# One accumulator for three float passes, and another order of the first units

## The chip, the cores and the metric

The kernel runs on one core of one Trainium2 chip. The metric is the time of one execution in microseconds (us), as the device counts it. Its parts are called by the names of the profile: PE is the matrix engine and PEld its weight loads, ACT, DVE and POOL are the engines that work element by element, SP issues nearly all the DMA transfers.

## The reference

A decaying linear attention over `q`, `k`, `v` (batch 4, 8 heads, 768 tokens, 64 columns a head) is worked in blocks of 64 tokens, with a state that runs from block to block. Its result, seen as 3072 tokens of 512 values, goes through two dense layers with a leaky rectifier between:

```
x = attn_out.transpose(0, 2, 1, 3).reshape(B * S, H * D)   # 3072 x 512
h = x @ w_in                                               # 512 x 2048
g = np.maximum(0.01 * h, h)
return (g @ w_out).astype(np.float32)                      # 2048 x 512
```

The two weight matrices arrive as 8-byte floats, the rest as 4-byte floats.

## The kernel before, in words

**Precision by three passes.** Every dense product is worked in three matmul passes over operands of a short float type. An operand `x` is cut into `xh` (rounded), `xl` (the rest) and `xm`; a weight is cut into `wh`, `wl` and `wm` the same way (`parts`, L587 to L598, and `difference`, L600). The passes are called h, l and m. With S = 4096, the product is (S+1) times (hh + ll), plus mm, all over S times U. So the sum of the first two passes must be multiplied by S+1 before or after the third is joined to it.

**Stage 1** (`up`, L628) works for a group `g` of 4 chunks of 128 tokens and one of 8 slices `p` of 256 columns of `w_in`: a unit `("up", g, p)`. A unit has two blocks of 128 columns, and a block has 4 matmuls of 512 columns for each pass, so a unit has 24 matmuls. Passes h and l add up in one bank of the accumulator memory (L655, L656). Then ACT multiplies the bank in place by S+1 (L658), pass m is added (L660), and ACT takes the bank through the leaky rectifier into `gs` (L661), which a DMA writes to memory (L664). The blocks go round two banks at first and then three, `b10`, `b11`, `b2`.

**Stage 2** (`down`, L688) reads those results back (`down_load`, L673: ACT L682, DVE L683 and L685 make the three parts), and for each group and each of its 4 blocks of 128 tokens (`tb`) adds up 16 slices of 128. Passes h and l go to one bank and pass m to another, so that the 4 blocks fill all 8 banks (`acc`, L668). At the end ACT takes the first bank into `tt`, scaled (L722), and DVE adds the second to it (L729). The output rows are written by L732. The last block of all takes its m pass in two halves of 256 columns, so that the first half can be emptied early.

**Attention** runs in rounds `("r", c)`, one for each chunk: transposes (L403), scores and states (L313 into `psc`), outputs (L313 into `po`), with DVE (L452, L459), POOL (L419, L423, L462) and ACT (L414, L415, L491) between. Its results become `xh` (ACT L507), `xl` and `xm` (DVE L508, L510).

**Weights.** `("wi", p)` loads one slice of `w_in` in two halves of 512 KB each (L566), and turns 8-byte floats into 4-byte floats in the one buffer `w32`: ACT L578, L580 and L582, DVE L584 and L585 for each half. `parts` then makes `wh` (ACT L591 or DVE L593, whichever the planner finds), `wl` (DVE L596) and `wm` (DVE L602). The next slice may be written to `w32` by L578 once the last reader of `w32` is through; before, that reader is `wl`, since `wm` is made of `wl` and `wh`. `w_out` goes the same way during stage 1, is parked in memory, and is cut into parts near the end of stage 1.

**The order.** `seq` (L738) is a list written out by hand for the first 41 entries, and made by loops afterwards. Its place in the list is an operation's rank. A planner (`Plan.emit`, L83) gives each operation a start by hand-written costs: whatever can start first goes first, and ranks decide between equals. Keys (the strings in `add`) carry the reads and writes between operations, in the order of `seq`. Each engine then runs its own instructions in the planned order and waits at the first that isn't ready. While the first units are not there yet, `busy` (L263) fills PE's idle time with transposes of an identity.

Of the kernel before, what the change touches and what calls it, by code (L numbers as in the profile page):

```python
# [8 lines left out]
F32 = mybir.dt.float32  # L9
# [6 lines left out]
ALU = mybir.AluOpType  # L16
# [9 lines left out]
S = 4096.0  # L26
NEAR = 1.0 - 2.0 ** -13
U = 16.0
WS = S * U
# [133 lines left out]
def kernel(  # L163
# [65 lines left out]
    tt = [raw[-1][:, i * T:(i + 1) * T] for i in range(2)]  # L229
# [357 lines left out]
    def parts(p, src, keys):  # L587
        wh, wl, wm = W[p]
        def head(e):
            if e == "ACT":  # L590
                nc.scalar.activation(out=wh, in_=src, func=AF.Copy, bias=0.0, scale=NEAR / S)  # L591
            else:
                nc.vector.tensor_scalar(wh, src, NEAR / S, None, op0=ALU.mult)  # L593

        add(("ACT", "DVE"), (1.05, 0.7), head, keys, [f"wh{p}"])
        add("DVE", 1.25, lambda: nc.vector.scalar_tensor_tensor(wl, wh.bitcast(F32), -S, src, op0=ALU.mult, op1=ALU.add),  # L596
            keys + [f"wh{p}"], [f"wl{p}"])
        difference(p)  # L598

    def difference(p):  # L600
        wh, wl, wm = W[p]
        add("DVE", 1.25, lambda: nc.vector.scalar_tensor_tensor(wm, wl.bitcast(F32), 1.0, wh.bitcast(F32), op0=ALU.mult, op1=ALU.subtract),  # L602
            [f"wh{p}", f"wl{p}"], [f"wm{p}"])
# [24 lines left out]
    def up(g, p, lo=0, hi=GC):  # L628
# [20 lines left out]
        for fs in blocks:  # L649
            kb = ("b10", "b2")[n_b % 2] if n_b < 0 else ("b10", "b11", "b2")[n_b % 3]  # L650
            n_b += 1
            b = bank[kb][:, :len(fs) * n].rearrange("p (f t) -> p f t", f=len(fs))
            r = y[:, fs[0]:fs[-1] + 1, :]
            for i, f in enumerate(fs):
                add("PE", us, lambda f=f, d=b[:, i, :], first=i == 0: product(d, f, 0, first), keys("h"), [kb])  # L655
                add("PE", us, lambda f=f, d=b[:, i, :]: product(d, f, 1), keys("l"), [kb])  # L656
            ns = 0.6 if len(fs) * n == T else 0.4
            add("ACT", ns, lambda b=b: nc.scalar.activation(out=b, in_=b, func=AF.Copy, bias=0.0, scale=S + 1.0), [], [kb], rank=-1.5)  # L658
            for i, f in enumerate(fs):
                add("PE", us, lambda f=f, d=b[:, i, :]: product(d, f, 2), keys("m"), [kb])  # L660
            add("ACT", ns, lambda b=b, r=r: nc.scalar.activation(out=r, in_=b, func=AF.Prelu, bias=0.0, scale=1.0 / WS, alpha=0.01),  # L661
                [kb], [f"gs{jg}"], rank=-1.5)
# [5 lines left out]
    acc = [[z[:, i].rearrange("p y t -> p (y t)") for i in range(2)] for z in (psc, po)] + [  # L668
        [b1[0], b2], [b1[1], pt.rearrange("p y t -> p (y t)")]]
    ACC = [["psc", "psc"], ["po", "po"], ["b10", "b2"], ["b11", "pt"]]  # L670
# [17 lines left out]
    def down(g, p):  # L688

        nonlocal n_t  # L690
        for tb in range(GC):
            done = p + 2 == NP
            very_last = done and g == NG - 1 and tb == GC - 1

            def go(pps, zs, cols, tb=tb):
                for pp in pps:
                    j = (g * NP + pp) % NR
                    for f in range(2):
                        for z in zs:
                            nc.tensor.matmul(acc[tb][z // 2][:, cols], lhsT=ring[j][z][:, f * T + tb * P:f * T + (tb + 1) * P],  # L700
                                             rhs=W[pp][z][:, f * d_model:(f + 1) * d_model][:, cols],
                                             start=pp == 0 and f == 0 and z != 1, stop=pp == NP - 1 and f == 1,
# [4 lines left out]

# [7 lines left out]
            for pps, zs, cols in order:  # L715
                part_of = f"{halves.index(cols)}" if cols in halves else ""
                add("PE", 0.227 * 2 * len(pps) * len(zs) * (0.53 if part_of else 1.0), lambda pps=pps, zs=zs, cols=cols, go=go: go(pps, zs, cols),
                    needs(pps, ["hlm"[z] for z in zs]) + ([ACC[tb][1]] if part_of else []), sorted({ACC[tb][z // 2] + part_of for z in zs}))
            if done:
                jt, n_t = n_t % 2, n_t + 1  # L720
                t, y = tt[jt], gs[jt][:, 0, :]
                add("ACT", 0.6, lambda t=t, tb=tb: nc.scalar.activation(out=t, in_=acc[tb][0], func=AF.Copy, bias=0.0, scale=(1.0 + 1.0 / S) / U),  # L722
                    [ACC[tb][0]], [f"t{jt}"], rank=-1.5)
                rows = out[(g * GC + tb) * P:(g * GC + tb + 1) * P, :]
                n = 2 if very_last else 1
                for i in range(n):
                    cols = slice(i * d_model // n, (i + 1) * d_model // n)
                    add("DVE", 0.69 / n + 0.08 * (n - 1),
                        lambda t=t, y=y, tb=tb, cols=cols: nc.vector.scalar_tensor_tensor(  # L729
                            y[:, cols], acc[tb][1][:, cols], 1.0 / WS, t[:, cols], op0=ALU.mult, op1=ALU.add),  # L730
                        [f"t{jt}", ACC[tb][1]] + ([ACC[tb][1] + str(i)] if n == 2 else []), [f"gs{jt}{i}" if n == 2 else f"gs{jt}"], rank=-1.5)
                    add("DMA", 0.8 / n, lambda rows=rows, y=y, cols=cols: nc.sync.dma_start(out=rows[:, cols], in_=y[:, cols]),  # L732
                        [f"gs{jt}{i}" if n == 2 else f"gs{jt}"], [], rank=-1.5)
# [4 lines left out]
    seq = [("a", 0), ("a", 1), ("a", 2), ("a", 3), ("wi", 1), ("b", 4), ("r", 4), ("up", 0, 1), ("wi", 0), ("r", 5),  # L738
# [24 lines left out]
    for n, x in enumerate(seq):  # L763
# [15 lines left out]
        elif x[0] == "wp":  # L779
            if not freed:  # L780
                add("DVE", 0.0, lambda: None, [], ATT + [f"gr{j}" for j in range(NR)])
                add("ACT", 0.0, lambda: None, [], [f"raw{j}" for j in range(NRAW)] + ["t0", "t1"])
# [38 lines left out]
```

## Time and profile before

| | |
|---|---|
| time, median of 3 runs | 612.35 us (611.60 to 612.74) |
| span of the profiled execution, first to last instruction | 609.2 us; no other time of that execution is recorded |
| mean granted TensorE clock | 0.999 |
| PE busy | 597.9 us, 5386 matmuls |
| ACT busy | 269.0 us, of it L658 56.1 us in 97 instructions |
| DVE busy | 314.0 us |
| first unit of stage 1 begins | 28.67 us |
| first matmul of stage 2 begins | about 343.5 us |
| last matmul ends | 605.62 us |

A profile row gives a line of the kernel, an engine and an operation with its tiles, how often it ran, its busy time and the mean of one, and behind the bar how long the engine stood idle before it and who ended that. "128x512" is 128 partitions by 512 elements. A matmul's record lasts longer than the step from one matmul to the next, since matmuls are pipelined; the step is what counts for the time.

### The profile page before, as it was taken

Reading aid. Unit: us, or ns where it says so; the run is one execution under the profiler, and the core shown is the slowest. Engines: PE = TensorE matmul, PEld = TensorE weight load, DVE = VectorE, ACT = ScalarE, POOL = GpSimd, SP = SyncE. Lnnn points to the kernel's source line nnn. Section 1 sums busy time; section 2 is a strip of 40 time slices with the busy share of each in tenths; the row PEclk is TensorE's granted clock in tenths of the full one; section 3 lists DMA queues with packets and bytes.
Section 4 is the critical chain, followed back from the end, with each engine's and each line's share of the span. In section 5 each row is a group of like instructions: output and inputs, shape, how many; then the busy total and the mean of one; then the engine's idle time right before and its main releaser. Section 6 shows DMA issues by size and latency. Waiting matters only on the chain.

```text
span 609.2 us, 12932 instructions
## 1 busy us (share of the span) xinstructions
PE 597.9 (98%) x5386; PEld 495.6 (81%) x5386; DVE 314.0 (52%) x418; ACT 269.0 (44%) x430; POOL 86.8 (14%) x90
## 2 busy tenths in 40 slices
PE   7899999999999999999999999999999999999997
PEld 6687888888888878888788888888888888888886
DVE  5999764334243426326366745545454544635531
ACT  4688974444455646555577522222222313214111
POOL 1654412104133004104000000000000000000000
PEclk9999999999999999999999999999999999999999
DMA  9998774667888878886686843524333343333201
GB/s 213 232 272 245 221 203 124 173 133 199 199 213 238 212 227 214 216 244 210 233 300 217 290 145 103 173 69 139 138 104 131 112 138 105 138 104 122 86 1 69
DMA packets 147754, 105.18 MB, mean 173 GB/s; under 512 B 123632, under 2 KB 124400, under 8 KB 147696
## 3 DMA queue, kind: packets, MB, share of 16 engines
q1 hardware_dynamic: 147552, 104.36, 58.9%
q8 instruction: 42, 0.69, 0.5%
q14 instruction: 16, 0.13, 0.1%
q10 hardware_dynamic: 144, 0.00, 0.0%
HBM read 68.69 MB, written 35.65 MB: 171 GB/s over the span
## 4 chain that ended last, share of the span: by engine, by line
PE 92%; DVE 4%; DMA 2%; ACT 1%; issue 0%; POOL 0%; SPq 0%; DVEq 0%; ACTq 0%
PE b L640 40%; PE b L700 18%; PE po L700 11%; PE psc L700 11%; PE po L313 4%; PE pt L700 4%; PE psc L313 4%; DMA g<-gs 1%; DMA att<-in_v_dram 1%; DVE w L584 1%; DVE w L585 1%; DVE wm L602 1%; PE pt L403 1%; DMA att<-in_k_dram 1%; DVE wl L596 0%; DVE wh L593 0%
## 5 line engine op out<-in xcount | busy, mean ns | idle before, releaser
L682 ACT ACTIVATE xh<-att 128x1024 fp32r<-128x1024 f32 x48 | 50.7, 1060 | 148.7 <-PE b L700 140.7
L683 DVE SCALAR_TENSOR_TENSOR xl<-att,xh 128x1024 fp32r<-128x1024 f32 x48 | 58.6, 1223 | 98.6 <-ACT xh L682 98.6
L640 PE MATMUL b<-xm,wm 128*128 128x512 f32 (+2 forms) x392 | 104.5, 393 | 0.5 <-ACT b L658 0.5
L640 PE MATMUL b<-xl,wl 128*128 128x512 f32 (+2 forms) x392 | 103.4, 388 | 0.6 <-DVE wl L596 0.6
L640 PE MATMUL b<-xh,wh 128*128 128x512 f32 (+2 forms) x392 | 103.2, 387 | 0.8 <-ACT xh L507 0.8
L640 PEld LDWEIGHTS b<-xh,wh 128*128 128x128 f32 x392 | 73.0, 188 | 15.9 <-ACT xh L507 0.9
L640 PEld LDWEIGHTS b<-xl,wl 128*128 128x128 f32 x392 | 72.8, 188 | 15.6 <-DVE wl L596 1.0
L640 PEld LDWEIGHTS b<-xm,wm 128*128 128x128 f32 x392 | 71.5, 188 | 15.7 <-ACT b L658 0.9
L658 ACT ACTIVATE b<-b 128x512 f32<-128x512 f32 (+2 forms) x97 | 56.1, 580 | 60.3 <-PE b L640 60.1
L661 ACT ACTIVATE gs<-b 128x512 f32<-128x512 f32 (+2 forms) x97 | 56.8, 591 | 44.9 <-PE b L640 38.8
L700 PE MATMUL b<-wl,xl 128*128 128x512 f32 x192 | 74.8, 390 | 0.0
L700 PE MATMUL b<-wh,xh 128*128 128x512 f32 x192 | 74.8, 390 | 0.0
L685 DVE SCALAR_TENSOR_TENSOR xm<-xl,xh 128x1024 fp32r<-128x1024 f32 x48 | 58.7, 1226 | 4.7
L462 POOL TENSOR_TENSOR att<-att 128x256 f32<-128x256 f32 x40 | 35.0, 876 | 57.2 <-DVE att L459 55.9
L700 PEld LDWEIGHTS b<-wl,xl 128*128 128x128 f32 x192 | 36.1, 188 | 7.4
L700 PEld LDWEIGHTS b<-wh,xh 128*128 128x128 f32 x192 | 36.0, 188 | 7.5
L423 POOL TENSOR_TENSOR att<-att 128x512 f32<-128x512 f32 (+1 forms) x20 | 24.2, 1211 | 96.2 <-DVE att L383 47.4
L452 DVE TENSOR_TENSOR att<-psc,att 128x512 f32<-128x512 f32 x24 | 16.5, 690 | 41.0 <-PE psc L313 41.0
L584 DVE TENSOR_SCALAR w<-w 128x512 int32<-128x512 int32 x32 | 19.2, 599 | 35.4 <-ACT w L578 35.3
L700 PE MATMUL po<-wm,xm 128*128 128x512 f32 x96 | 37.4, 390 | 0.0
L700 PE MATMUL po<-wh,xh 128*128 128x512 f32 x96 | 37.4, 390 | 0.0
L700 PE MATMUL po<-wl,xl 128*128 128x512 f32 x96 | 37.4, 390 | 0.0
(73 smaller groups left out, 805.4 us busy)
## 6 DMA issues: line engine op xcount, KB each, us to landing
att<-g SPq DMA_DIRECT2D x48, 512.0 KB, 3.3
g<-gs SPq DMA_DIRECT2D x47, 512.0 KB, 4.0
raw<-in_moe_w_in_dram SPq DMA_DIRECT2D x16, 512.0 KB, 5.4
raw<-in_moe_w_out_dram SPq DMA_DIRECT2D x16, 512.0 KB, 4.7
att<-in_k_dram SPq DMA_DIRECT2D x48, 128.0 KB, 4.2
att<-in_v_dram SPq DMA_DIRECT2D x24, 256.0 KB, 4.4
out_dram<-gs SPq DMA_DIRECT2D x23, 256.0 KB, 2.1
wo<-w SPq DMA_DIRECT2D x8, 512.0 KB, 5.9
```

The lines of the kernel that those rows point to most:

```text
L313: nc.tensor.matmul(dst[HALF[cols]], lhsT=lhsT[HALF[rows]], rhs=rhs[HALF[rows]], start=start, stop=True, skip_group_check=True)
L423: add(eng, us, lambda: e.tensor_tensor(o, x, _bc(pow_q, 2, 2)[:, :, m, :], op=ALU.mult), ["fq", dep], [f"qsT{i}"])
L452: add("DVE", 0.69, lambda: nc.vector.tensor_tensor(sc, psc[:, :, lower, :], decay, op=ALU.mult), ["psc", "fk"], ["sc"])
L462: add("POOL", 0.7, lambda new=new, j=j: nc.gpsimd.tensor_tensor(state[(j + 1) % 4], new, _bc(lam_c, 2, D), op=ALU.mult), [f"st{j % 4}", "f ...
L584: add("DVE", 0.42, lambda: nc.vector.tensor_scalar(d, d, 3, None, op0=ALU.logical_shift_left), [], [key])
L640: nc.tensor.matmul(dst, lhsT=w[z][:, kk * 2 * P + f * P:kk * 2 * P + (f + 1) * P], rhs=x[z][:, kk, toks], start=start and kk == 0, stop=kk ...
L658: add("ACT", ns, lambda b=b: nc.scalar.activation(out=b, in_=b, func=AF.Copy, bias=0.0, scale=S + 1.0), [], [kb], rank=-1.5)
L661: add("ACT", ns, lambda b=b, r=r: nc.scalar.activation(out=r, in_=b, func=AF.Prelu, bias=0.0, scale=1.0 / WS, alpha=0.01), [kb], [f"gs{jg} ...
L682: add("ACT", 1.05, lambda: nc.scalar.activation(out=h, in_=graw[j], func=AF.Copy, bias=0.0, scale=NEAR), reads, wr("h"))
L683: add("DVE", 1.25, lambda: nc.vector.scalar_tensor_tensor(l, graw[j], 1.0, h.bitcast(F32), op0=ALU.mult, op1=ALU.subtract), reads + [f"rh{ ...
L685: add("DVE", 1.25, lambda: nc.vector.scalar_tensor_tensor(m, l.bitcast(F32), -S, h.bitcast(F32), op0=ALU.mult, op1=ALU.add), [f"rh{j}", f" ...
L700: nc.tensor.matmul(acc[tb][z // 2][:, cols], lhsT=ring[j][z][:, f * T + tb * P:f * T + (tb + 1) * P], rhs=W[pp][z][:, f * d_model:(f + 1) ...
```

## The change

The factor S+1 is moved into the third part of the weight: `wm` becomes source/(S+1) minus `wh`. Then all three passes add up in one bank, and one scale OUT = (S+1)/(S·U) is applied when the bank is emptied. In stage 1 the ACT instruction between the passes goes. In stage 2 a block of tokens has one bank instead of two, banks alternate between even and odd groups, and the ACT and DVE pair that emptied two banks becomes one instruction on either engine. The hand-written part of `seq` is ordered anew.

```diff
-WS = S * U
+OUT = (S + 1.0) / (S * U)
...
-    tt = [raw[-1][:, i * T:(i + 1) * T] for i in range(2)]
...
-        difference(p)
-
-    def difference(p):
-        wh, wl, wm = W[p]
-        add("DVE", 1.25, lambda: nc.vector.scalar_tensor_tensor(wm, wl.bitcast(F32), 1.0, wh.bitcast(F32), op0=ALU.mult, op1=ALU.subtract),
-            [f"wh{p}", f"wl{p}"], [f"wm{p}"])
+        add("DVE", 1.25, lambda: nc.vector.scalar_tensor_tensor(wm, src, 1.0 / (S + 1.0), wh.bitcast(F32), op0=ALU.mult, op1=ALU.subtract),
+            keys + [f"wh{p}"], [f"wm{p}"])
...
-            add("ACT", ns, lambda b=b: nc.scalar.activation(out=b, in_=b, func=AF.Copy, bias=0.0, scale=S + 1.0), [], [kb], rank=-1.5)
             for i, f in enumerate(fs):
                 add("PE", us, lambda f=f, d=b[:, i, :]: product(d, f, 2), keys("m"), [kb])
-            add("ACT", ns, lambda b=b, r=r: nc.scalar.activation(out=r, in_=b, func=AF.Prelu, bias=0.0, scale=1.0 / WS, alpha=0.01),
+            add("ACT", ns, lambda b=b, r=r: nc.scalar.activation(out=r, in_=b, func=AF.Prelu, bias=0.0, scale=OUT, alpha=0.01),
...
-    acc = [[z[:, i].rearrange("p y t -> p (y t)") for i in range(2)] for z in (psc, po)] + [
-        [b1[0], b2], [b1[1], pt.rearrange("p y t -> p (y t)")]]
-    ACC = [["psc", "psc"], ["po", "po"], ["b10", "b2"], ["b11", "pt"]]
+    acc = [z[:, i].rearrange("p y t -> p (y t)") for z in (psc, po) for i in range(2)] + [
+        pt.rearrange("p y t -> p (y t)"), b1[0], b1[1], b2]
+    ACC = ["psc", "psc", "po", "po", "pt", "b10", "b11", "b2"]
+    ACC = [x + str(i % 2) if x in ("psc", "po") else x for i, x in enumerate(ACC)]
...
+            a = g % 2 * GC + tb
+            bank_a, key = acc[a], ACC[a]
...
-                            nc.tensor.matmul(acc[tb][z // 2][:, cols], lhsT=ring[j][z][:, f * T + tb * P:f * T + (tb + 1) * P],
+                            nc.tensor.matmul(dst[:, cols], lhsT=ring[j][z][:, f * T + tb * P:f * T + (tb + 1) * P],
                                              rhs=W[pp][z][:, f * d_model:(f + 1) * d_model][:, cols],
-                                             start=pp == 0 and f == 0 and z != 1, stop=pp == NP - 1 and f == 1,
+                                             start=pp == 0 and f == 0 and z == 0, stop=pp == NP - 1 and f == 1,
...
-                add("ACT", 0.6, lambda t=t, tb=tb: nc.scalar.activation(out=t, in_=acc[tb][0], func=AF.Copy, bias=0.0, scale=(1.0 + 1.0 / S) / U),
-                    [ACC[tb][0]], [f"t{jt}"], rank=-1.5)
...
-                    add("DVE", 0.69 / n + 0.08 * (n - 1),
-                        lambda t=t, y=y, tb=tb, cols=cols: nc.vector.scalar_tensor_tensor(
-                            y[:, cols], acc[tb][1][:, cols], 1.0 / WS, t[:, cols], op0=ALU.mult, op1=ALU.add),
...
+                    def evac(e, y=y, cols=cols, src=bank_a):
+                        if e == "ACT":
+                            nc.scalar.activation(out=y[:, cols], in_=src[:, cols], func=AF.Copy, bias=0.0, scale=OUT)
+                        else:
+                            nc.vector.tensor_scalar(y[:, cols], src[:, cols], OUT, None, op0=ALU.mult)
...
+                    add(("ACT", "DVE"), (0.6 / n + 0.1 * (n - 1), 0.69 / n + 0.08 * (n - 1)), evac,
...
-    seq = [("a", 0), ("a", 1), ("a", 2), ("a", 3), ("wi", 1), ("b", 4), ("r", 4), ("up", 0, 1), ("wi", 0), ("r", 5),
-           ("wi", 2), ("wi", 3), ("up", 0, 0), ("up", 0, 2), ("up", 0, 3), ("r", 6), ("up", 1, 1, 0, 3), ("r", 7),
-           ("wi", 4), ("up", 0, 4), ("wi", 7), ("up", 1, 1, 3, 4), ("up", 1, 3), ("up", 0, 7), ("up", 1, 2),
-           ("wi", 6), ("up", 0, 6), ("wi", 5), ("ls",), ("up", 0, 5), ("r", 8), ("lt",), ("up", 1, 7), ("r", 9),
-           ("up", 1, 4), ("r", 10), ("up", 1, 0), ("r", 11), ("up", 1, 6), ("up", 1, 5)]
+    seq = [("a", 0), ("a", 1), ("a", 2), ("a", 3), ("wi", 1), ("b", 4), ("up", 0, 1), ("wi", 0), ("wi", 2), ("r", 4),
+           ("wi", 3), ("r", 5), ("up", 0, 0), ("up", 0, 2), ("r", 6), ("wi", 4), ("r", 7), ("wi", 6), ("up", 0, 3),
+           ("up", 1, 1, 0, 3), ("wi", 5), ("up", 0, 4), ("up", 1, 3), ("up", 0, 5), ("up", 1, 2), ("wi", 7),
+           ("up", 0, 6), ("up", 0, 7), ("ls",), ("r", 8), ("up", 1, 0), ("lt",), ("r", 9), ("up", 1, 5), ("r", 10),
+           ("up", 1, 4), ("r", 11), ("up", 1, 6), ("up", 1, 7), ("up", 1, 1, 3, 4)]
```

More of the change, by code (lines that the diff above doesn't have):

```diff
@@ L693, in down, with go @@
             very_last = done and g == NG - 1 and tb == GC - 1
-            def go(pps, zs, cols, tb=tb):
+            a = g % 2 * GC + tb
+            bank_a, key = acc[a], ACC[a]
+            whole = [key] + ([key[:-1]] if g == 0 and key[:-1] in ("psc", "po") else [])
+            def go(pps, zs, cols, tb=tb, dst=bank_a):
                 for pp in pps:
@@ L717, in down @@
                 add("PE", 0.227 * 2 * len(pps) * len(zs) * (0.53 if part_of else 1.0), lambda pps=pps, zs=zs, cols=cols, go=go: go(pps, zs, cols),
-                    needs(pps, ["hlm"[z] for z in zs]) + ([ACC[tb][1]] if part_of else []), sorted({ACC[tb][z // 2] + part_of for z in zs}))
+                    needs(pps, ["hlm"[z] for z in zs]) + ([key] if part_of else []), [key + "h" + part_of] if part_of else whole)
             if done:
                 jt, n_t = n_t % 2, n_t + 1
-                t, y = tt[jt], gs[jt][:, 0, :]
-                add("ACT", 0.6, lambda t=t, tb=tb: nc.scalar.activation(out=t, in_=acc[tb][0], func=AF.Copy, bias=0.0, scale=(1.0 + 1.0 / S) / U),
-                    [ACC[tb][0]], [f"t{jt}"], rank=-1.5)
+                y = gs[jt][:, 0, :]
                 rows = out[(g * GC + tb) * P:(g * GC + tb + 1) * P, :]
@@ L727, in down @@
                     cols = slice(i * d_model // n, (i + 1) * d_model // n)
-                    add("DVE", 0.69 / n + 0.08 * (n - 1),
-                        lambda t=t, y=y, tb=tb, cols=cols: nc.vector.scalar_tensor_tensor(
-                            y[:, cols], acc[tb][1][:, cols], 1.0 / WS, t[:, cols], op0=ALU.mult, op1=ALU.add),
-                        [f"t{jt}", ACC[tb][1]] + ([ACC[tb][1] + str(i)] if n == 2 else []), [f"gs{jt}{i}" if n == 2 else f"gs{jt}"], rank=-1.5)
-                    add("DMA", 0.8 / n, lambda rows=rows, y=y, cols=cols: nc.sync.dma_start(out=rows[:, cols], in_=y[:, cols]),
-                        [f"gs{jt}{i}" if n == 2 else f"gs{jt}"], [], rank=-1.5)
-    seq = [("a", 0), ("a", 1), ("a", 2), ("a", 3), ("wi", 1), ("b", 4), ("r", 4), ("up", 0, 1), ("wi", 0), ("r", 5),
[4 rows of a table removed]
+                    def evac(e, y=y, cols=cols, src=bank_a):
[3 more added lines that the diff above has]
+                            nc.vector.tensor_scalar(y[:, cols], src[:, cols], OUT, None, op0=ALU.mult)
+                    gk = f"gs{jt}{i}" if n == 2 else f"gs{jt}"
+                    add(("ACT", "DVE"), (0.6 / n + 0.1 * (n - 1), 0.69 / n + 0.08 * (n - 1)), evac,
+                        [key] + ([key + "h" + str(i)] if n == 2 else []), [gk] + ([f"gs{jt}"] if n == 2 and i == 0 else []), rank=-1.5)
+                    add("DMA", 0.8 / n, lambda rows=rows, y=y, cols=cols: nc.sync.dma_start(out=rows[:, cols], in_=y[:, cols]),
+                        [gk], [], rank=-1.5)
+    seq = [("a", 0), ("a", 1), ("a", 2), ("a", 3), ("wi", 1), ("b", 4), ("up", 0, 1), ("wi", 0), ("wi", 2), ("r", 4),
[4 rows of a table added]
     nxt, n_out, begin = 3 * GC, 0, len(seq)
@@ L781 @@
                 add("DVE", 0.0, lambda: None, [], ATT + [f"gr{j}" for j in range(NR)])
-                add("ACT", 0.0, lambda: None, [], [f"raw{j}" for j in range(NRAW)] + ["t0", "t1"])
+                add("ACT", 0.0, lambda: None, [], [f"raw{j}" for j in range(NRAW)])
                 freed = True
```

## The prediction

> **What bounds the kernel now.** I first cut the span at the marks of the kernel (first unit at 28.6 us, stage 2 from 343.5, last matmul at 605.6) and asked for the busy time of each engine in each stretch:
>
> ```profile
> core 0: us, PE busy (x) PEld busy (x) DVE busy (x) ACT busy (x) POOL busy (x), PEclk, DMA share, GB/s
> 0.00:28.60 28.60, 22.73 (x566) 18.17 (x566) 20.45 (x46) 15.95 (x29) 11.27 (x19) 1.00 0.96 220
> 28.60:62.00 33.40, 32.27 (x537) 26.76 (x537) 31.86 (x41) 26.72 (x49) 17.52 (x13) 1.00 0.93 262
> 62.00:343.50 281.50, 280.74 (x3127) 233.53 (x3126) 132.39 (x213) 162.82 (x283) 58.03 (x59) 1.00 0.76 212
> 343.50:605.60 262.10, 262.10 (x1161) 217.16 (x1159) 128.58 (x118) 63.50 (x72) 0.00 (x0) 1.00 0.34 116
> ```
>
> From 28.6 us on PE is busy nearly all the time: 32.27 of 33.40, then 280.74 of 281.50, then all of it. The other engines are half idle, except in the second stretch, where DVE is at 31.86 of 33.40 and the DMA engines at 0.93. Second view, the list of everything that PE waited for:
>
> ```profile
> PE psc L313 <- DVE att L459: 1.8, 2, 1.1
> PE b L266 <- POOL att L269: 1.4, 1, 1.4
> PE psc L313 <- DMA att<-in_v_dram: 0.9, 1, 0.9
> PE b L640 <- ACT xh L507: 0.8, 1, 0.8
> PE b L640 <- DVE wl L596: 0.6, 1, 0.6
> PE b L640 <- ACT b L658: 0.5, 1, 0.5
> ...
> PE po L403 <- DVE xl L508: 0.4, 1, 0.4
> PE po L313 <- ACT att L491: 0.3, 1, 0.3
> ```
>
> The columns are total us, times, longest. The line to see is the sixth: the ACT scaling between the passes, which the change removes, made PE wait once in 97 times, 0.5 us. Third, the scaling itself in the groups:
>
> ```profile
> L658 ACT ACTIVATE b<-b 128x512 f32<-128x512 f32 (+2 forms) x97 | 56.1, 580 | 60.3 <-PE b L640 60.1
> L661 ACT ACTIVATE gs<-b 128x512 f32<-128x512 f32 (+2 forms) x97 | 56.8, 591 | 44.9 <-PE b L640 38.8
> ```
>
> 56.1 us of ACT, but ACT waited 60.1 us for PE here, and not the other way. Fourth, the chain of work that ended last, in order of time, gives PE's step:
>
> ```profile
> 597.41 2.72 PE po L700 x12
> 600.13 4.53 PE b L700 x20
> ```
>
> 4.53 us over 20 matmuls is 226.5 ns, whichever bank is written. The dense layers have 2 x 1152 matmuls of 512 columns, that is 2304 x 0.2265 = 522 us. The change adds and removes no matmul. So what can be won is PE's idle time alone, and what can be lost is new idle time.
>
> Start to start in the timeline, PE's four stops after 28.67 us cost more than the idle column says, since a record is longer than a step: 30.39 to 31.22 (0.60 over the step, DVE `xl`), 46.40 to 47.40 (0.77, DVE `wl`), 222.79 to 223.66 (0.65, the ACT scaling) and 0.45 at 298 (ACT L491). Together 2.5 us. Other small losses, some 7 us between 28.7 and 343 us, are steps of 0.1 us where PE changes between attention and dense work; those changes stay.
>
> **The change, part by part.**
>
> *The scaling in stage 1 goes.* Sure gain: the stop at 223.66, 0.65 us. ACT stood there behind L661, which waited for a DMA to free `gs`, and pass m stood behind ACT. After, ACT can be as late, but PE only meets it when a bank comes round again, two blocks (2 x 12 x 0.227 = 5.4 us) later. What is late next: nothing there. All other 96 scalings were hidden under the other block's passes, so they are worth nothing by themselves: 0 to 0.2 us.
>
> *What ACT's free time does early.* From 28.6 to 62 us, 8 scalings took 4.69 us of ACT's 26.72. In the same stretch DVE made three of the four `wh` (L593, 3.4 us in all) because ACT was behind; a fourth on ACT took 1.06 us (L591). If ACT takes all, 3 x 1.06 = 3.2 us fits in the 4.69 freed, and DVE falls from 31.86 to about 28.5 of 33.4. Then the stops on `wl` (0.77) and on `xl` (0.60) can go. Bounds: 0 to -1.37 us. I take -1.05: all of the first, half of the second, whose place at 31 us is too early for much relief.
>
> *The third weight part.* Same engine, same shape; its neighbour L596 reads the same two operands (a 4-byte source and `wh`) at 1.21 to 1.23 us where L602 took 1.22, so the instruction costs the same, within 0.02 us. But it now reads `w32`, so the next slice's L578 must wait for `wm` instead of `wl`. At 47.38 the trace shows ACT already held 0.80 us at L578 by `wl`; `wm` ended at 49.81, and DVE took L584 of the next slice at 49.72. After, L578 (0.66) begins at 49.81 and L584 at about 50.57: 0.85 us later. Behind the waiting L578 on ACT stand `xh` (L507) and the rectifier, which PE needs. Four slices in the stretch: between 0 (DVE has attention work in between) and 3.4 us. Later slices come 10 us apart (L596 at 65.8, 74.9, 84.0, 94.6) and hide it. I take 0, because the relief of 3.4 us on DVE is of the same size, and keep 3.4 for the range. For `w_out` the buffers are four deep and DVE is half idle: 0.
>
> *Stage 2.* Out go 24 ACT copies of 0.6 us (L722) and 25 DVE adds of 0.69 (L729); in come 25 of 0.6 or 0.69 on one of the two. PE never waited there (262.10 of 262.10), so the gain is 0. Banks come round after two groups (87 us) instead of one, so no wait can come of it. If both engines were late, the price would appear at a change of group; I see no row for it. A step into one bank for all three passes costs the same: stage 1 writes h and l to one bank at 227 ns.
>
> *The tail.* The last matmul ended at 605.62, the two halves on DVE ran from 605.71 to 606.47, and the rest to 609.24 is transfers and the end. The ACT copy before it was hidden. After, two halves go to ACT or DVE: the nearest rows are 0.37 us for 128x256 (L658's shortest) and 0.41 to 0.43 (L729). Bounds: -0.4 (one half on each engine) to +0.1. I take 0.
>
> *The reordered units.* No work is added. The slices 2, 3, 4 and 6 move ahead, the rounds 4 to 7 back, and with them their loads on SP's one queue: 512 KB halves (5.4 us to landing) go ahead of 128 KB of `k` and `q` and 256 KB of `v` (4.1 to 4.5 us) while the DMA engines are at 0.93. The first unit's inputs (chunks 0 to 3, slice 1, chunks 4 and 5) keep their places, so 28.67 stays. A slice gives PE 24 x 0.227 = 5.45 us for about 5.5 us of DVE (L584 2 x 0.42, L585 2 x 0.69, L593 0.7, L596 and L602 1.22 each, sums to 5.4), a round some 3 us for 3 us. As neither order gives PE more work per us of DVE, I take 0; bounds -1 (the prologue's waits of 1 us each shift) to +4.6 (the two stretches of attention that filled PE at 33.57 to 35.19 and 40.79 to 43.77 come too late).
>
> **Sum.** -0.65 - 1.05 = -1.7 us on the span of 609.2, so 607.5. The median of the runs lies 3.1 us above that span (the record has no other time for the profiled execution), and I keep the 3.1: 612.35 - 1.7 = 610.65, rounded to **610.6 us**.
>
> [...] Row first: the granted clock is 1.00 in every stretch up to the last matmul, and PE's longest listed wait is 1.4 us. [...]
>
> **Rivals.**
>
> *Nothing to be had* (612.35, within 1.2 us either way). The change does not do what it seems: L658 was hidden 96 times in 97, and DVE, not ACT, limits the early stretch. ACT's time is freed, DVE keeps `wh`, the stops move to other places. For it: the waits list. Against it: 0.65 us is certain, and ACT was at 0.80 in that stretch.
>
> *Slower: the single buffer `w32` becomes the pacemaker.* With `wm` as the last reader, one slice's chain in sequence is L578 0.66, L584 and L585 twice 1.11, `wh` 1.06, `wl` 1.22, `wm` 1.22, together 6.4 us, where it was 5.2 with `wm` beside the next slice's start. A unit feeds PE 5.45. Where slices 0, 2 and 3 follow one another with the rounds ranked behind, PE starves 0.95 us for each: 2.9 us, less the 0.65: **614.6**. It decides as soon as the chain is longer than PE's work between two units, that is, if less than one round's PE work (about 3 us) stands ready each time. For it: DVE is at 31.86 of 33.40, and PE already waited for `wl` there. Against it: PE had rounds in between before, and the planner takes whatever can start.
>
> *A larger gain* (608.5): the waits before 28.67, 5.6 us in the list, shrink too, or all four stops go (-2.5) with 0.4 in the tail and 1 in the prologue. Nothing that feeds the first unit is changed, so this is the least likely.
>
> **How the numbers follow.** Forecast with its larger form: -1.2 to -4 us, 0.50 (0.08 of it the larger gain). Nothing to be had: 0.22. Slower: 0.28. A measurement tells 0.2% (1.2 us) from no change, so faster 0.50, same 0.22, slower 0.28. The range leaves out half of the larger gain, and beyond the rival at 614.6 only the upper part of the unknown price of the order: 608.4 to 615.0. The forecast's own range is 609.4 to 611.3.
>
> **What would show it.** Right: no wait of PE on an ACT scaling; `wh` mostly on ACT (L591's line) before 62 us; DVE under 0.9 in that stretch; stage 2 at 226.5 ns a step; first unit near 28.7. Wrong: PE waits on `wl`, `wm` or L578's successors between 34 and 100 us, adding to more than 2 us; a first unit at another time; a step in stage 2 other than 227 ns, which would overthrow the whole sum.

## The result, and the profile after

The changed kernel takes 625.78 us, median of 4 runs (623.86 to 626.94). The kernel before took 611.98 us beside it (4 runs, 611.39 to 612.74). The ratio is 1.0224, interval 1.0202 to 1.0246: slower by 13.8 us, where 610.6 us was forecast and 615.0 was the end of the range. The profiled execution took 625.05 us, its span is 622.8, so 2.2 us lie around the span. Line numbers move by one to six: L640 is now L635, L661 is L655, L700 is L698, and L722 and L729 are one line, L726.

From the page after, first the PE, DVE and ACT totals, then the group of the one ACT instruction that is left for each bank of stage 1:

```profile
PE 603.4 (97%) x5386; PEld 497.1 (80%) x5386; DVE 298.5 (48%) x392; ACT 215.9 (35%) x335; POOL 83.4 (13%) x90
...
L655 ACT ACTIVATE gs<-b 128x512 f32<-128x512 f32 (+2 forms) x97 | 57.5, 594 | 149.7 <-PE b L635 139.3
```

The work did go: ACT has 53 us less to do, DVE 15.5 less, and PE has the same 5386 matmuls. ACT now stands 139.3 us waiting for PE in that group. The time it saved became waiting, and PE is still what everything waits for. The last three of the prediction's four stretches, cut beside the changed kernel's own marks (first unit 29.09, stage 2 from 351.87, last matmul begins at 619.0):

```profile
core 0: us, PE busy (x) PEld busy (x) DVE busy (x) ACT busy (x) POOL busy (x), PEclk, DMA share, GB/s
28.60:62.00 33.40, 32.48 (x455) 26.45 (x459) 31.40 (x41) 24.36 (x42) 14.06 (x12) 1.00 0.96 273
62.00:351.70 289.70, 284.52 (x3224) 236.31 (x3216) 134.57 (x216) 112.96 (x195) 58.51 (x61) 0.99 0.73 207
351.70:619.30 267.60, 263.30 (x1158) 216.04 (x1156) 112.80 (x94) 62.28 (x70) 0.00 (x0) 1.00 0.33 112
```

The loss is in two places. Stage 2, which was busy to the last hundredth, took 262.0 us from first to last matmul and now takes 267.1. The stretch from 62 us to stage 2 has PE idle for 5.2 us where it had 0.8, and a granted clock of 0.99 instead of 1.00. The first stretch looks as before. What PE waited for (us in total, times, longest):

```profile
PE po L698 <- ACT gs L726: 2.2, 3, 0.7
PE psc L312 <- DVE att L382: 2.1, 1, 2.1
...
PE psc L698 <- ACT gs L726: 2.1, 3, 0.7
...
PE b L635 <- DVE wl L595: 1.0, 1, 1.0
PE po L312 <- DVE att L490: 1.0, 1, 1.0
```

**Stage 2.** Two of these lines are new: six stops on the ACT instruction that empties a bank. The timeline round the first of them (start, duration, in brackets the idle time before and who ended it):

```profile
388.36 0.39 PE L698 MATMUL psc<-wm,xm 128*128 128x512 f32 x1
...
389.44 0.50 PE L698 MATMUL psc<-wh,xh 128*128 128x512 f32 x1 [0.69 <-ACT gs L726]
```

The last matmul of a block begins at 388.36, and the next matmul begins 1.08 us later instead of 0.2265. That next matmul belongs to the next block. Its bank is free, but the bank is part of the same tile `psc` that L726 is reading. The stops lie at 388.4, 394.8, 477.4, 483.9, 566.5 and 572.9: two in each even group, whose four blocks use `psc`, `psc`, `po`, `po`. The odd groups use tiles of one bank each and have none. Six times 0.87 over the step is 5.2 us.

**The late stop of stage 1.** The other new piece is near 180 us. First what PE, DVE and SP did there:

```profile
175.62 0.47 SPq L373 DMA_DIRECT2D att<-in_q_dram  x1
...
178.27 0.65 PE L312 MATMUL psc<-att 64*64 64x64 f32 x32
...
179.63 0.77 DVE L382 STREAM_TRANSPOSE att<-raw 128x256 f32<-128x256 f32 x2 [10.41 <-DMA att<-in_q_dram]
...
181.05 0.69 PE L312 MATMUL psc<-att 64*64 64x64 f32 x32 [2.13 <-DVE att L382]
...
182.75 0.70 PE L312 MATMUL po<-att 64*64 64x64 f32 x16 [1.00 <-DVE att L490]
...
183.38 2.07 PE L635 MATMUL b<-xl,wl 128*128 128x512 f32 x4
```

The rounds from number 10 on get `k` and `q` in lists of small transfers (L373, 32 or 48 KB each). SP issues them one by one, each taking 0.47 us of SP, among the loads of `w_out` and the writes of stage 1. The last `q` transfer for the round that PE has reached is issued at 175.62 and lands at 179.6. DVE had waited 10.41 us for it, and PE waits behind DVE's transposes. In the kernel before, the last transfer of that list was issued at 171.93, and DVE began at 173.75, a good 3 us before PE came to the round's scores at 177.21. Its transposes ended at 175.70, so the slack was 1.5 us:

```profile
171.93 0.47 SPq L374 DMA_DIRECT2D att<-in_q_dram  x1
...
173.75 0.77 DVE L383 STREAM_TRANSPOSE att<-raw 128x256 f32<-128x256 f32 x2 [4.88 <-DMA att<-in_q_dram]
174.44 1.26 DVE L383 STREAM_TRANSPOSE att<-att 128x512 f32<-128x512 f32 x2
...
177.21 1.11 PE L313 MATMUL psc<-att 64*64 64x64 f32 x64
```

And the stop costs more than its idle time. Busy times of the changed kernel in steps of 4 us, with columns as above:

```profile
178.00:182.00 4.00, 1.61 (x96) 1.33 (x87) 2.37 (x5) 1.95 (x3) 0.93 (x1) 1.00 1.06 325
182.00:186.00 4.00, 3.25 (x22) 2.65 (x23) 3.71 (x8) 0.60 (x1) 1.82 (x3) 0.51 0.97 312
186.00:190.00 4.00, 4.00 (x13) 3.11 (x13) 1.63 (x4) 0.60 (x1) 2.25 (x3) 0.63 0.04 14
```

After the stop the granted clock is 0.51. The 12 dense matmuls from 183.38 to 188.67 took 5.29 us instead of 12 x 0.2265 = 2.72. Start to start, over the steps, PE lost some 7 us between 175 and 200 us, against less than 1 before: 6.3 us more.

From the first matmul's start to the last one's, the same 5386 matmuls took 604.0 us before and 617.6 after: 13.6 of the 13.8. Stage 2 and the late stop make 11.5 of it. Of the rest, 0.7 is two stops near 65 us in place of two that went, and 0.4 the later first unit; about 1 us is spread over small steps.

### The profile page after: what moved, and what is told of

Same layout as the page of the kernel before. It is cut to its first block, busy times and chain, and to the rows that moved or that the text cites. A ratio compares the mean times of both kernels' runs of the same rounds, so it can differ in the third digit from the quotient of the medians.

```text
span 622.8 us, 12771 instructions
## 1 busy us (share of the span) xinstructions
PE 603.4 (97%) x5386; PEld 497.1 (80%) x5386; DVE 298.5 (48%) x392; ACT 215.9 (35%) x335; POOL 83.4 (13%) x90
## 4 chain that ended last, share of the span: by engine, by line
PE 87%; DVE 7%; issue 2%; DMA 1%; ACT 1%; SPq 0%; ACTq 0%; DVEq 0%
PE b L635 38%; PE b L698 16%; PE psc L698 11%; PE po L698 11%; PE pt L698 5%; PE po L312 3%; PE psc L312 3%; DVE w L584 1%; DMA raw<-in_moe_w_in_dram 1%; DVE wm L597 1%; DVE w L583 1%; DVE wl L595 1%; ACT gs L726 1%; DVE wh L592 1%; DMA att<-in_k_dram 1%
## 5 line engine op out<-in xcount | busy, mean ns | idle before, releaser
L655 ACT ACTIVATE gs<-b 128x512 f32<-128x512 f32 (+2 forms) x97 | 57.5, 594 | 149.7 <-PE b L635 139.3
L635 PE MATMUL b<-xh,wh 128*128 128x512 f32 (+2 forms) x392 | 105.3, 392 | 1.5 <-ACT xh L506 0.8
L635 PE MATMUL b<-xl,wl 128*128 128x512 f32 (+2 forms) x392 | 105.5, 392 | 1.0 <-DVE wl L595 1.0
L635 PE MATMUL b<-xm,wm 128*128 128x512 f32 (+2 forms) x392 | 105.0, 390 | 0.0
L635 PEld LDWEIGHTS b<-xl,wl 128*128 128x128 f32 x392 | 73.1, 190 | 16.8 <-DVE wl L595 1.9
L635 PEld LDWEIGHTS b<-xh,wh 128*128 128x128 f32 x392 | 72.8, 189 | 16.8 <-ACT xh L506 0.9
L635 PEld LDWEIGHTS b<-xm,wm 128*128 128x128 f32 x392 | 73.1, 189 | 15.4 <-DVE wm L597 0.3
L698 PE MATMUL b<-wh,xh 128*128 128x512 f32 x144 | 56.0, 389 | 0.0
L698 PE MATMUL b<-wl,xl 128*128 128x512 f32 x144 | 56.0, 389 | 0.0
L698 PE MATMUL b<-wm,xm 128*128 128x512 f32 (+1 forms) x148 | 55.6, 383 | 0.0
L698 PE MATMUL po<-wh,xh 128*128 128x512 f32 x96 | 37.7, 393 | 2.2 <-ACT gs L726 2.2
L461 POOL TENSOR_TENSOR att<-att 128x256 f32<-128x256 f32 x40 | 32.7, 819 | 52.6 <-DVE att L458 49.1
L698 PE MATMUL psc<-wh,xh 128*128 128x512 f32 x96 | 37.7, 393 | 2.1 <-ACT gs L726 2.1
L583 DVE TENSOR_SCALAR w<-w 128x512 int32<-128x512 int32 x32 | 17.6, 550 | 45.4 <-ACT w L577 45.3
L698 PE MATMUL psc<-wl,xl 128*128 128x512 f32 x96 | 37.4, 389 | 0.0
L698 PE MATMUL po<-wm,xm 128*128 128x512 f32 x96 | 37.4, 389 | 0.0
L698 PE MATMUL psc<-wm,xm 128*128 128x512 f32 x96 | 37.3, 389 | 0.0
L698 PE MATMUL po<-wl,xl 128*128 128x512 f32 x96 | 37.3, 389 | 0.0
```

Source lines behind the costliest of these rows:

```text
L461: add("POOL", 0.7, lambda new=new, j=j: nc.gpsimd.tensor_tensor(state[(j + 1) % 4], new, _bc(lam_c, 2, D), op=ALU.mult), [f"st{j % 4}", "f ...
L583: add("DVE", 0.42, lambda: nc.vector.tensor_scalar(d, d, 3, None, op0=ALU.logical_shift_left), [], [key])
L635: nc.tensor.matmul(dst, lhsT=w[z][:, kk * 2 * P + f * P:kk * 2 * P + (f + 1) * P], rhs=x[z][:, kk, toks], start=start and kk == 0, stop=kk ...
L698: nc.tensor.matmul(dst[:, cols], lhsT=ring[j][z][:, f * T + tb * P:f * T + (tb + 1) * P], rhs=W[pp][z][:, f * d_model:(f + 1) * d_model][: ...
```

## Experiments

In each, "excess" is the median less the median of the kernel before on the same chip at the same time.

### Three edits, one by one

**The changed kernel with the old list** (`seq` as before, all else changed).

> The changed kernel with the old list of first units; all else of the change stays. Theory (the new order alone loses the 8.5 us of stage 1, by the stop at 178.7 us and the half clock after it; stage 2 loses its own 5.2): stage 2 begins 8 us earlier, near 344 us, and the time falls from 625.8 to about 617.5. Rival (the order is innocent; taking the scaling out lets the planner shift the transfers on SP's queue): stage 2 still begins near 351 us, the time stays within 2 us of 625.8.

622.45 us against 611.75, ratio 1.0186 (1.0160 to 1.0213), excess 10.7. The old list gives back only 3.1 of 13.8. Stage 2 still began late (351.3), so the order is not what delays stage 1 in the main.

**The kernel before with the new list** (only `seq` is new).

> The kernel before with the new list of first units, and nothing else of the change. Theory (the order alone costs stage 1's loss): 612.0 plus 8, about 620, with a stop of PE between 170 and 190 us. Rival (the order is innocent): 612.0 within 1.5 us.

615.84 us against 611.75, ratio 1.0099 (1.0064 to 1.0133), excess 4.1. The list costs about this much by itself. Its stops were at 43.7 (0.68 us over the step), 64.8 (1.84), 85.8 (1.25) and 146.6 (0.89), and one of 0.6 stood at 180.6, at the same transposes as the late stop. In that profile the mean clock was 0.999, as in the kernel before, but two of the five executions took 619.7 and 620.0 us, at mean clocks of 0.997 and 0.993. So 4.1 is the price at a mean clock of 0.999, and the interval reaches to 8.

**Neighbouring blocks in different tiles.**

```diff
-    acc = [z[:, i].rearrange("p y t -> p (y t)") for z in (psc, po) for i in range(2)] + [
+    acc = [z[:, i].rearrange("p y t -> p (y t)") for i in range(2) for z in (psc, po)] + [
...
-    ACC = ["psc", "psc", "po", "po", "pt", "b10", "b11", "b2"]
-    ACC = [x + str(i % 2) if x in ("psc", "po") else x for i, x in enumerate(ACC)]
+    ACC = ["psc0", "po0", "psc1", "po1", "pt", "b10", "b11", "b2"]
```

> The changed kernel with the banks of an even group dealt out as psc0, po0, psc1, po1 instead of psc0, psc1, po0, po1, so that two blocks in a row never use banks of the same tile. Theory (a matmul into the second bank of a tile waits until ACT has emptied the first bank of the same tile, though the banks are apart): the six stops of 0.85 to 0.90 us in stage 2 go, 5.2 us less, about 620.6. Rival (a block's bank is emptied too late in itself): the six stops stay at other banks, 625.8 within 1 us.

620.76 us against 611.75, ratio 1.0149 (1.0113 to 1.0186), excess 9.0. No instruction is added or taken away, two banks only change places. The six stops are gone, and stage 2 is busy throughout:

```profile
353.40:614.70 261.30, 261.30 (x1157) 216.54 (x1155) 112.64 (x94) 62.60 (x70) 0.00 (x0) 1.00 0.33 114
```

So the tile, not the bank, is what the matmul waited for.

**Both: old list and banks apart.**

> The changed kernel with both: the old list of first units and the banks dealt out apart. Theory (order 8.5 us and tiles 5.2 us add up and are all of the loss): 612 to 612.5, and 0.65 below the kernel before if the stop on the scaling was a true price, 611.4. Rival (the folding itself costs something in stage 1): 614 or more.

616.88 us against 611.75, ratio 1.0104 (1.0073 to 1.0134), excess 5.1. What is left of the change here is the folding in stage 1: no scaling, and `wm` made from the source. That alone costs 5.1. Two of its stops are those that the slower rival of the prediction names: ACT's L577 waits for `wm` before it may write `w32`, and then PE waits for `wl`:

```profile
48.73 2.12 PE L635 MATMUL b<-xl,wl 128*128 128x512 f32 x8 [0.87 <-DVE wl L595]
...
49.84 1.23 ACT L577 ACTIVATE w<-raw 128x512 f32<-128x512 f32 x2 [1.86 <-DVE wm L597]
...
58.79 2.11 PE L635 MATMUL b<-xl,wl 128*128 128x512 f32 x8 [1.18 <-DVE wl L595]
...
60.33 1.23 ACT L577 ACTIVATE w<-raw 128x512 f32<-128x512 f32 x2 [2.59 <-DVE wm L597]
```

But 1.03 and 1.34 us over the step are 2.4 of 5.1. The others stand at 144.3 (0.89), 179.6 (0.94) and 181.0 (1.17): rounds again.

### Inside the folding

These four start from the last kernel (old list, banks apart).

**`wm` made of `wl` and `wh` again**, so that `w32` comes free early. The division of the third part by S+1 is left out here.

```diff
-        add("DVE", 1.25, lambda: nc.vector.scalar_tensor_tensor(wm, src, 1.0 / (S + 1.0), wh.bitcast(F32), op0=ALU.mult, op1=ALU.subtract),
-            keys + [f"wh{p}"], [f"wm{p}"])
+        add("DVE", 1.25, lambda: nc.vector.scalar_tensor_tensor(wm, wl.bitcast(F32), 1.0, wh.bitcast(F32), op0=ALU.mult, op1=ALU.subtract),
+            [f"wh{p}", f"wl{p}"], [f"wm{p}"])
```

> The kernel with the old order and the banks apart (616.9 against 611.75 before), with one edit: wm is made of wl and wh again, as before the change, so that the 4-byte weights in w32 are free after wl. (wm is then too large by S+1, so the third pass has a wrong scale.) Theory A (what is left of the loss, 5.1 us, is w32's later release: ACT stood 1.86 and 2.59 us at L577 for wm, and PE then 1.03 and 1.34 us at wl): both stops of PE on wl shrink to one of 0.8 or less, stage 2 begins near 344 to 345, time 612 to 613.5. Theory B (the loss comes from taking the scaling out, which moves the planner's places for attention and for SP's transfers, seen as the stops at 144 and 180 us): 616 to 617, with the stops at 144 and 180 still there.

621.41 us against 611.41, ratio 1.0176 (1.0133 to 1.0219), excess 10.0: worse, not better. The early stops on `wl` are gone, and one of 3.9 us for a `v` stands at 142.4, with a granted clock of 0.91 over the stretch from 120 to 160 us:

```profile
146.36 1.98 PE L312 MATMUL psc<-att 64*64 64x64 f32 x64 [3.76 <-DMA att<-in_v_dram]
```

SP issued that `v` at 142.55, behind 31 small list transfers (from 123.8 to 141.4). My theory, that the later release of `w32` is all of stage 1's loss, fell here.

**An ACT copy in place between the passes**, as long as the old scaling, that changes nothing.

```diff
+            add("ACT", ns, lambda b=b: nc.scalar.activation(out=b, in_=b, func=AF.Copy, bias=0.0, scale=1.0), [], [kb], rank=-1.5)
```

> The kernel with the old order and the banks apart, with an ACT copy in place by 1.0 put back between the passes of stage 1, so that the planner sees as many operations as before the change; wm still reads w32. Theory A (w32's release): no gain, 616 to 618, ACT still stands at L577 for wm. Theory B (taking the scaling out is what costs): 612 to 613.

614.32 us against 611.41, ratio 1.0052 (1.0032 to 1.0072), excess 2.9. With 97 instructions more, the kernel is faster: the stops at 144 and 180 are gone. Early ones remain, at 54.6 (1.39), 57.0 (1.13) and 91.6 (0.95).

**Both put back**: the copy, and `wm` of `wl` and `wh` (again without the division by S+1).

> Both edits together: the copy between the passes, and wm of wl and wh (again with the wrong scale of the third pass). Stage 1 is then the kernel before in all but constants; what is left of the change is one bank for a block in stage 2, with the banks apart. Both theories: 611.75 within 1 us, since stage 2 had no stop before. If it is slower by more, stage 2's single bank costs something that I have not seen.

611.11 us against 611.41, ratio 0.9995 (0.9983 to 1.0008): the time of the kernel before. Its single bank in stage 2 costs and gains nothing. From this kernel to the one above it the edit differs only in what `wm` reads: 3.2 us, close to the 2.9 that the rival reckoned. But the planner answered that edit with another order: 180 of PE's 5386 matmuls stand in other places, the first of them the 811th, and so do SP's transfers. So 3.2 is the price of the later release and of that order together; no run here parts them. Without the copy, freeing `w32` early had cost 4.9 us instead of saving 3.2. The two parts of the folding don't add up.

**The second part from the third**: `wm` first, then `wl` from `wm` and `wh`, passes in the order h, m, l. Nothing is left out, and `w32` comes free early.

```diff
...
+        add("DVE", 1.25, lambda: nc.vector.scalar_tensor_tensor(wl, wm.bitcast(F32), S + 1.0, wh.bitcast(F32), op0=ALU.mult, op1=ALU.add),
+            [f"wh{p}", f"wm{p}"], [f"wl{p}"])
...
```

> The kernel with the old order and the banks apart, with the folding kept but the parts made in another order: wm of w32 and wh first, then wl = (S+1) wm + wh, so that w32 is free after the first of the two; stage 1's passes run h, m, l. Nothing is left out. Theory A (w32's release is the loss): as the run with wm of wl, 612 to 613.5, or 611 if the stop on the scaling was a true price. Theory B: 616 to 617.

622.70 us against 611.41, ratio 1.0192 (1.0170 to 1.0214), excess 11.3, with a stop of 5.0 us for `v` at 142.8. It repeats the finding of the third part made of the second.

### The instruction, or the plan

**A planned step without an instruction.** The planner gets the copy's cost and keys and orders everything as if it were there; ACT gets nothing to do. The order on PE, DVE, POOL and SP is that of the kernel with the copy.

```diff
+            add("ACT", ns, lambda: None, [], [kb], rank=-1.5)
```

> The kernel with the old order and the banks apart (616.9), in which the planner still reckons with an ACT step of 0.6 us between the passes of stage 1 but no instruction is issued for it. PE, DVE, POOL and SP then run the same instructions in the same order as in the run with the real copy (614.3), ACT 97 fewer. Theory (it is the order in which the planner places attention rounds and units, not the missing instruction, that made the kernel slower): 614 or a little less, 613 to 614.5, no stop between 140 and 190 us, and the stop on the copy near 223 us gone. Rival (an ACT with fewer instructions runs ahead and harms the transfers or the banks): 616 or more.

615.00 us against 610.64, ratio 1.0066 (1.0040 to 1.0091), excess 4.4. Taking 97 instructions of 56 us off ACT in an unchanged order gains nothing; the interval overlaps that of the copy itself (1.0032 to 1.0072). No stop is left between 140 and 190 us, but there is one early:

```profile
58.43 2.04 PE L635 MATMUL b<-xh,wh 128*128 128x512 f32 x7 [2.93 <-DVE wh L592]
```

Against the kernel without the step (1.0073 to 1.0134) the intervals overlap too: with the old list the plan's share can't be told from nothing.

**The same step with `w32` freed early** (the second part from the third).

> The same planned-only step, old order, banks apart, and the weight parts made so that w32 is free after the first of the two (wm from w32, then wl from wm; passes h, m, l). Nothing is left out of the computation. Theory (w32's release costs 3.2 us, the order of the planner the rest): both gone, 610 to 611.5, at or just under the kernel before. Rival (the parts' new order brings its own cost, as in the run at 622.7): 613 or more.

615.83 us against 610.64, ratio 1.0077 (1.0055 to 1.0099), excess 5.2. It came from 11.3, but not to zero: stops of its own at 64.3 (1.70), 143.9 (1.37) and 146.5 (1.41).

**The same step with the new list**, banks apart.

> The changed kernel with the banks apart (620.8) and its new list of units, with the planned-only step between the passes. Theory (the new list costs some 4 us by itself, as on the kernel before, and w32's release 3): 616 to 619, the stop at 180 us smaller than 2.3. Rival (the new list was made for the order without the step and only fits that): 620 or more.

615.27 us against 610.64, ratio 1.0066 (1.0043 to 1.0090), excess 4.6, where the same kernel without the step has 9.0, and here the intervals are apart. The stop at 180 is gone. A step that issues no instruction at all moves 4.4 us. So with this list the plan alone makes about half of the 9.0. The copy itself was not tried with this list.

**The new list with `w32` freed early**, without the step.

> The changed kernel with the banks apart and its new list of units (620.8), with the parts in the order that frees w32 early, no planned-only step. Theory A (w32's release costs PE about 2 us at 63 to 67 us here, and the rest comes from the rounds' places): 618 to 619, the two stops at 63 to 67 gone, the stop near 180 still there. Rival (freeing w32 early makes it worse without the planned step, as in the old order, by 5 us): 624 or more.

619.00 us against 610.64, ratio 1.0131 (1.0110 to 1.0152), excess 8.4. The stops at 63 to 67 us are gone, one at 84 (1.08) has come, and the late one (2.98 and 1.17) stays. The release of `w32` isn't the cause of the late stop.

### The late stop

These test why the list of `q` is late at 180 us with the new list and banks apart (excess 9.0).

**Stage 1's writes from ACT's queue** instead of SP's (L658), in case SP stands there waiting for ACT.

> The changed kernel with the banks apart and its new list (620.8), with the writes of stage 1's results issued from ACT's queue, where they follow the rectifier that makes them, instead of SP's. PE, DVE and POOL keep their instructions and order. Theory A (SP's one queue stands at these writes and the attention loads behind them come too late, so PE stops near 180 us): the stop shrinks from 2.5 plus 0.8 us to under 1, the granted clock stays at 1.0, 615 to 617. Rival (the transfers of that round are late for another reason: they are issued one by one, 0.47 us each, after their buffers come free): the stop near 180 stays over 2 us, 619.5 to 622.

621.79 us against 611.41, ratio 1.0161 (1.0140 to 1.0183), excess 10.4. The stop grew to 5.1 us: the theory fell.

**The late `q` lists from ACT's queue.**

```diff
-                        move(0.55, lambda o=o, z=z: nc.sync.dma_start(
+                        move(0.55, lambda o=o, z=z, e=(nc.scalar if nm == 'q' and c >= 15 else nc.sync): e.dma_start(
...
```

> The same kernel with the 16-transfer lists of q for the rounds from 15 on issued from ACT's queue, the k halves from SP's. PE, DVE and POOL keep their order. Theory (the stop near 180 is the wait for the last of these transfers, which SP issues until 177.8 us at 0.47 us each): the list is out some 6 us earlier, the stop near 180 goes or falls under 0.5 us, no half clock between 178 and 190 us, 614 to 616. Rival (the buffer of q comes free too late, whoever issues): the stop stays over 1.5 us, 619.5 to 622.

613.92 us (9 runs) against 611.41, ratio 1.0042 (1.0028 to 1.0055), excess 2.5. The order on PE, DVE and POOL is unchanged, and only these transfers have another issuer. The stop is gone, and the granted clock is 1.00 here:

```profile
178.00:182.00 4.00, 4.00 (x138) 3.33 (x137) 2.87 (x6) 3.09 (x5) 2.17 (x2) 1.00 0.60 167
182.00:186.00 4.00, 4.00 (x19) 3.33 (x18) 3.91 (x8) 0.73 (x2) 1.18 (x3) 1.00 0.96 288
```

The gain is 6.5 us, against 6.3 read from the changed kernel's timeline. What is left are the stops at 63 to 67 us, on `wh` (0.91) and `wl` (1.21), and a lower clock there: of the profile's 40 slices, the one from 61.2 to 76.5 us has a granted clock of 0.8 to 0.9, and every other 0.9 or more. From 62 to 71 us PE lost 4.0 us over its steps, against 0.1 in the kernel before. Less the two stops that went (0.77 and 0.65), that is the 2.5.

**Late rounds ranked ahead** by 6 places, with the old list and banks apart.

```diff
-        plan.rank = float(n)
+        plan.rank = float(n) - (6.0 if x[0] == 'r' and x[1] >= 8 else 0.0)
```

> The kernel with the old list and the banks apart (616.9), in which the attention rounds from 8 on get a rank lower by 6 in the planner, so that they win ties against units. Theory (without the step between the passes, the planner runs 156 unit matmuls between rounds 7 and 8 where the kernel before runs 76, and so the later rounds and their loads are late): round 8 moves from 109 to about 90 us, the stops at 144 and 180 shrink, 613.5 to 615.5. Rival (the rounds' place does not matter, their inputs are late): 616.5 or more.

619.13 us against 611.41, ratio 1.0117 (1.0090 to 1.0144), excess 7.7 where 5.1 was. Round 8 came only from 108 to 99 us, not to 90 as expected. Of the pair at 180 us, 0.4 was left, and another pair came at 267 and 268 us (0.84 and 1.32), and from 270 to 274 us the granted clock was 0.62. So moving the rounds this far moved the stops and did not take them away.

**The kernel before with its writes on ACT's queue**, a control.

> The kernel before with the writes of stage 1's results issued from ACT's queue. PE keeps its order. Theory A (SP's waits at these writes, 14.2 us between 62 and 200 us, cost the kernel before nothing, as PE is fed): 610.5 to 612.5. Rival (they cost 1 to 2 us in the early stretch, where PE stops on wl at 47 us): 609 to 610.

617.26 us against 611.41, ratio 1.0098 (1.0078 to 1.0117), excess 5.9. Neither expectation holds. The kernel before has nothing of the change, and yet gets a stop of 3.04 us at 178.6 behind the same transposes (L383), and others at 231.9 (1.32) and 272.0 (1.01). Its slack of 1.5 us at this place hangs on where SP's other transfers stand.

**The new list, `w32` freed early and the `q` lists on ACT's queue.**

> The changed kernel with its new list, the banks apart, the lists of q from round 15 on from ACT's queue (613.9), and the parts made so that w32 is free early (wm first, wl from wm, passes h, m, l). Nothing is left out. Theory (what is left of the loss, 2.5 us, is the two stops of 0.9 and 1.2 us at 63 to 67 us, for wh and wl behind w32's release): these go, 610.5 to 612. Rival (early freeing brings other stops of the same size, one near 84 us as in the run without the ACT queue): 613 or more.

614.23 us against 611.10, ratio 1.0051 (1.0039 to 1.0064), excess 3.1, no better than with `wm` from the source. The stops at 63 to 67 us are gone, and others have come: 83.4 (1.10), 143.1 (0.89), 178 to 180 (0.53 and 1.17). So the last 2.5 to 3 us have a place in each of these two kernels, but no single cause that I could show. Why one stop comes where another goes stays open.

**The kernel before with its `q` lists on ACT's queue**, a control.

> The kernel before with the same lists of q from ACT's queue, as a control. Theory (the kernel before has no stop near 180, so nothing is gained): 611.4 within 1 us. Rival (the lists from ACT help by themselves): 609 to 610, and then the 6.8 us gained on the changed kernel are not all the stop's.

610.37 us (11 runs) against 611.10 (15 runs), ratio 0.9984 (0.9974 to 0.9994). Of the 6.5 us above, about 0.7 (0.4 to 1.6) is a gain that has nothing to do with the change. It is also the fastest kernel of the study, by 0.16%.

## Why the prediction was wrong

On the path from the kernel before to the one after, by excess: the folding in stage 1 gives 5.1 us (old list, banks apart), the new list 3.9 more (9.0), and the shared tiles 4.8 more (13.8). The intervals of the first two steps overlap (1.0073 to 1.0134 and 1.0113 to 1.0186), so their division is rough; that of the tiles is clear of them (1.0202 to 1.0246).

- **"PE's idle time alone can be won" and "the other 96 scalings were hidden"**: right. The stop on the scaling went, and so did 56 us of ACT's work, and it was worth nothing (planned step against copy).
- **"Stage 2 ... the gain is 0 ... no wait can come of it"**: the first failing step, 4.8 to 5.2 us. I looked at when the same bank comes round. I didn't look at which tile the next block's bank lies in. Before, the two banks of `psc` were one block's, so a matmul never followed an ACT read of the other half. The step from matmul to matmul is 227 ns as forecast.
- **"If ACT takes all, 3 x 1.06 ... I take -1.05"**: failed. `wh` stayed on DVE (L592) except for the first slice, and DVE has 31.40 of 33.40. The stop at 46.4 went, and stops of 0.90 and 1.20 us on `wh` and `wl` came at 63.6 and 65.4.
- **The release of `w32`, "between 0 and 3.4 us, I take 0"**: failed. The waits stand where the rival put them (48.73 and 58.79), and they go when `w32` comes free early. With the copy between the passes, release and order together cost 3.2 us; without it, freeing `w32` early brought larger stops elsewhere. The term leaned on DVE being relieved by 3.4 us, which did not happen.
- **"The reordered units ... I take 0; bounds -1 to +4.6"**: the bound held, the value didn't. The list costs 4.1 alone and 3.9 on top. The reason given, some 5.4 us of DVE for a slice, took L584 at 0.42 and L593 at 0.7, their shortest; from 28.6 to 62 us their medians were 0.63 and 1.26, which makes 6.3 us, more than the 5.45 that a slice gives PE.
- **Not priced at all**: that removing a step from the plan moves other work. With the old list, PE did 76 unit matmuls between rounds 7 and 8 and 120 between 8 and 9; without the step, 156 and 36. Rounds come later or closer together, their lists on SP's one queue come due in other places, and in the changed kernel that is the stop at 180 us with a granted clock of 0.51 and 0.63 in the steps of 4 us behind it, 6.3 us. It goes by a planned step alone, and by another issuer for the `q` lists in an unchanged order on PE, DVE and POOL. I looked at ACT and DVE up to 100 us, and at SP's queue only there.
- **The slower rival** had the right sign and one right mechanism, at 2.9 us. The largest terms lay outside it, so the range ended 10.8 us too low.
- **First unit (29.1 against 28.7) and the tail (3.9 us from the last matmul's start to the end, as before)**: as forecast.

## What to carry to other kernels

Here one engine was busy for 97% of the span, and removing hidden work from another gained nothing; the question is what new waits the new order makes. Where a planner orders the work, an instruction's removal should be costed in two parts, the instruction and its place in the plan; a planned step that issues nothing tells them apart. Before two accumulators alternate, look whether they lie in one tile, and before work is moved, look how much slack the last transfer of each list has on its queue.

## What the runs showed of the hardware

**The clock.** PE began 32 small matmuls at 178.27, 32 more at 181.05 and 16 at 182.75. From 183.38 to 188.67 dense matmuls went at 427 ns or more a step, where the step is 226.5 ns elsewhere; the 12 of them lost 2.6 us. The trace of the changed kernel holds the granted clock: 1.00 up to 182.10, 0.50 from there to 188.93, and 1.00 again. Cut there (columns as above):

```profile
178.10:182.10 4.00, 1.51 (x88) 1.23 (x80) 2.47 (x5) 1.95 (x3) 1.02 (x1) 1.00 1.06 323
182.10:188.92 6.82, 6.17 (x29) 4.90 (x30) 5.24 (x11) 1.19 (x2) 3.97 (x5) 0.50 0.57 188
188.92:192.92 4.00, 4.00 (x19) 3.26 (x19) 0.00 (x0) 0.60 (x1) 0.00 (x0) 1.00 0.15 61
```

The prediction's row, a granted clock of 1.00 beside a longest wait of 1.4 us, says nothing of this: that wait stood before PE's first matmul, which began at 1.36 us.

Two other pairs of stops differ in what came after them. Near 180 us in the kernel with the old list and banks apart, losses of 0.94 and 1.17 us, 1.5 us apart, left the clock at 1.00. With the late rounds ranked ahead, losses of 0.84 and 1.32 us, about as close together, were followed by 0.62. First the former, then the latter:

```profile
178.00:182.00 4.00, 2.46 (x114) 1.84 (x113) 2.88 (x5) 2.22 (x4) 1.27 (x1) 1.00 0.79 237
182.00:186.00 4.00, 3.77 (x31) 3.13 (x32) 3.90 (x10) 1.20 (x2) 2.23 (x3) 1.00 0.96 343
...
266.00:270.00 4.00, 2.19 (x121) 1.91 (x125) 3.50 (x6) 3.54 (x7) 1.27 (x1) 1.00 0.62 205
270.00:274.00 4.00, 4.00 (x26) 3.14 (x23) 3.97 (x9) 0.60 (x1) 2.45 (x3) 0.62 1.05 370
```

So stops of one size cost more in one run than in another, and what decides it was not shown. The two near 65 us stand in the same order of work in the changed kernel and with banks apart. Between 62 and 71 us PE lost 2.4 us in the first profile, where the granted clock was 1.00 from 62 to 70, and 3.9 in the second, whose slice from 61.8 to 77.3 us has a granted clock of 0.8 to 0.9. Nor is it the kernel alone: of the nine executions with the `q` lists on ACT's queue, the three at a mean clock of 1.00 took 612.4 to 612.6 us and the six at 0.997 took 613.5 to 614.9.

**Two issuers.** 48 transfers of 48 KB or less, at 0.47 us of SP each, given to ACT's queue, brought 6.5 us with the new list and 0.7 in the kernel before. There the list's last transfer had slack, and here it had none.
